# A row and its mirror image in one pass: first product shared between rows n and S-n, with the matmul order written out by hand

## The chip, the cores and the metric

The kernel runs on one core of a Trainium2 chip. A core has five engines, each with its own instruction queue that is served in order: PE (TensorE, matrix products; its weight loads are listed apart as PEld), DVE (VectorE), ACT (ScalarE), POOL (GpSimd) and SP (SyncE, which here only issues DMAs). Matrix products are written to PSUM, which has eight banks of 512 float32 columns in each of 128 partitions; everything else works from SBUF. The metric is the device time of one execution in microseconds; smaller is better.

## The reference

Input `x` is 8 batches of S = 3136 rows by 256 channels in float32. A two-dimensional Fourier transform is taken of each batch, and its real part goes through a mixer:

```
X = np.fft.fft(np.fft.fft(x, axis=1), axis=2).real      # rows, then channels
h = X.transpose(0, 2, 1) @ U @ V                         # rank 32 over the rows
u = X + h.transpose(0, 2, 1)
out = u + np.maximum(u @ w_ch1, 0) @ w_ch2               # 256 -> 1024 -> 256
```

For real input, X of row S-n is X of row n with the channels reversed (channel k and channel 256-k exchanged). The kernels use that.

## The kernel before, in words

**Layout.** Channels lie on partitions, rows on the free axis. Channels 1 to 127 and their mirror images 129 to 255 are kept as two halves of 128 partitions, so X of a batch is two tiles, `S` and `T`, of 128 partitions by 1569 columns: rows 0 to 1568 only. For row n the lower half is `S[:, n]` and the upper half `T[:, n]`; for row S-n the two change places. `W1[:, 0, :]` and `W1[:, 1, :]` hold the rows of `w_ch1` for the two halves (the second in the mirrored order).

**Transform of a batch** (`transform`, lines 669 to 678). `fold(b)` forms sums and differences of the loaded rows: DVE and POOL work in nine steps, of which `along_d` (L371, L373), `mirror` (L381, L384), `half` (L389) and `fourth` (L393) are the DVE ones. `load_x` brings the next batch into `xf` and `xr`, which exist once. Then come eight `seq` steps (L451): matmuls of 98 or 99 rows against cosine and sine tables into a PSUM tile of tag `dft`. In the first of each pair ACT copies the PSUM tile away (L467), in the second DVE combines it with that copy into `A` or `B` (`join`, L498 to L509; a POOL instruction, L512, turns the sign of one partition of `B`). Eight `chan` steps follow (two matmuls of 392 columns each, L567 and L569, and an ACT copy into `S` or `T`, L574), then `lowrank` (four matmuls of 256 columns, and two ACT copies into `TA`) and `mirror_row` (two DVE instructions on one partition, L588 and L590).

**The mixer** goes over all 25088 rows in 49 chunks of 512. `front(c)` adds the rank-32 part: two matmuls on 64 rows each of `TA` and `VA` (`s=0` on partitions 0 to 63, `s=1` on 64 to 127), into two PSUM tiles of tag `dft`; DVE adds `S` or `T` (L622) and writes `u`; a DMA from SP transposes `u` into `ut` (L625). `first_product(c, j)`, for j = 0 to 7, is two matmuls of 512 columns into a PSUM tile of tag `p1` and one ACT relu into `h` (L634, L636). `second_product(c, t)`, for t = 0 to 3, is eight matmuls of 256 columns into PSUM (tag `p2`, two t in one tile), after each pair three DVE adds with `ut` into `o` (L656, L658, L659), and after the fourth t a store of 512 rows.

**PSUM.** Of the eight banks, tag `dft` has three, `p1` three and `p2` two.

**Order.** Everything up to chunk 0, j = 3, with `front(1)` as its last step, is in the order of the text (`manual_schedule`). From there (`order.close()`, L851) a planner puts the instructions of each engine in order by its own estimate of when they are ready. The loop at L848 gives it, for each j of each chunk, first `first_product(c, j)`, then a tile of `second_product(c-1)`, then the steps of `transform(b)` due at that place (`due`); a batch's steps are spread evenly over the chunks of the batch before it. Chunk 0 begins once the first half of batch 0's `S` and `T` is there; `fold(1)` is the first thing that DVE does after the hand-ordered part.

**Set-up.** Before the loop: tables of sines and cosines, the transform of U, batch 0's transform, and the constants. POOL issues the loads of V into `VA`, clears its other rows (L199, L763), and casts `w_ch1` (L782).

Of the kernel before, what the change touches and what calls it, by code (L numbers as in the profile page):

```python
# [16 lines left out]
P = 128  # L17
# [14 lines left out]
def kernel(  # L32
# [16 lines left out]
    NCH = B * S // CH  # L49
# [48 lines left out]
    BUFS = {"dft": 3, "p1": 3, "p2": 2}  # L98
# [4 lines left out]
    UA = cpool.tile([KP, 4, NI, R], FP32, name="ua")  # L103
    J = cpool.tile([KP, KP], FP32, name="jx")
    jv = cpool.tile([KP, KP], FP32, name="jv")
    UR = cpool.tile([KP, 4, NI, R], FP32, name="ur")
    xidx = cpool.tile([P, B, 4], I32, name="xidx")
    krow = cpool.tile([P, 4 * NT], FP32, name="krow")
    kev = cpool.tile([P, 2 * NT], FP32, name="kev")
# [21 lines left out]
    lrow = cpool.tile([P, 2, P], FP32, name="lrow")  # L131
# [38 lines left out]
    VA = [cpool.tile([P, S], BF16, name=f"va{s}", tag=f"va{s}") for s in range(2)]  # L170
    TA = [cpool.tile([P, P], BF16, name=f"ta{s}", tag=f"ta{s}") for s in range(2)]
    MSN = cpool.tile([P, 256], BF16, name="msn")
    MC = cpool.tile([P, 256], BF16, name="mc")
    wp = ctx.enter_context(tc.tile_pool(name="wp", bufs=2))
    setup = ExitStack()
    gen = setup.enter_context(tc.tile_pool(name="gen", bufs=2))
# [14 lines left out]
    def cosine(out_, y, bits):  # L191
        pp = y.shape[0]
        ab = gen.tile(list(y.shape), FP32, tag="ab", name="ab")
# [4 lines left out]
    for r in (R, 3 * R):  # L198
        nc.gpsimd.memset(VA[0][r:r + R].bitcast(I32), 0)  # L199
# [5 lines left out]
    uy = cpool.tile([KP, 2, 2, 2, NI * R], FP32, name="uy")  # L205
    ueven = cpool.tile([KP, 2, 2, NI * R], FP32, name="ueven")
    GUO = cpool.tile([KP, 2, 2, NI, R], BF16, name="guo")
    GUC = [cpool.tile([KP, 2, NI, R], BF16, name=f"guc{c}", tag=f"guc{c}") for c in range(2)]

    NUO = cpool.tile([KP, 2, 2, R], BF16, name="nuo")  # L210
    NUC = [cpool.tile([KP, 2, R], BF16, name=f"nuc{c}", tag=f"nuc{c}") for c in range(2)]
# [185 lines left out]

    def fold(b):
# [50 lines left out]
    def add_up(pt, mm):  # L449
        for n, (at, w, rhs) in enumerate(mm):  # L450
            nc.tensor.matmul(pt[:, at:at + rhs.shape[-1]], w, rhs, start=(n == 0),  # L451
                             stop=(n == len(mm) - 1), skip_group_check=True)

    def seq(b, par, typ, pn, tag="dft", part=True):
# [5 lines left out]
        mm = products(b, par, typ, P * typ, pn == 1, ne)  # L460
        if typ == 0:
            mm = mm + products(b, par, 1, 256, (pn == 1) == (par == 1), ne)
        add_up(pt, mm)
# [51 lines left out]
    def seq_both(b, typ, tag, between):  # L515
# [3 lines left out]
        for pn in range(2):  # L519
            mm = products(b, 0, typ, P * typ, pn == 1, 0)  # L520
            if typ == 0:
                mm = mm + products(b, 0, 1, 256, pn == 0, 0)
            for n, (at, w, rhs) in enumerate(mm):
                nc.tensor.matmul(pt[:, at:at + rhs.shape[-1]], w, rhs, start=(pn == 0 and n == 0),
                                 stop=(n == len(mm) - 1), skip_group_check=True)
# [17 lines left out]
    def u_alone(b, typ, kept):  # L543
# [3 lines left out]
        mm = []  # L547
        for t, col in ((1, P),) if typ else ((0, 0), (1, 256)):
            for c in range(2):
                g = GC[b % 2][0 if (c == 0) == (t == 1) else 1]  # L550
                lo = TE - NT + NE * c
                mm += [(g[:kp(i), i, col:col + P], TABE[t][:kp(i), i, lo:lo + NE]) for i in range(NI)]
            for i in range(NI):
                tab, lo = (TABS[t], off_u(t, i)) if i % 2 else (TABO[t], 2 * NT)
                mm += [(GO[b % 2][:kp(i), nm, i, col:col + P], tab[:kp(i), nm, i // 2, lo:lo + NE])
                       for nm in range(2)]
        for n, (w, rhs) in enumerate(mm):
            nc.tensor.matmul(kept["pt"][:, typ, :], w, rhs, start=(n == 0), stop=(n == len(mm) - 1))
# [3 lines left out]
    def chan(b, ch, h, tag="dft"):  # L562
# [4 lines left out]
        nc.tensor.matmul(pt[:, :hi - lo], MC[:, h * P:(h + 1) * P], d["A"][:, lo:hi],  # L567
                         start=True, stop=False)
        nc.tensor.matmul(pt[:, :hi - lo], MSN[:, h * P:(h + 1) * P], d["B"][:, lo:hi],  # L569
                         start=False, stop=True)  # L570
# [5 lines left out]
    def lowrank(b):  # L576
        d = ST[b]
        pt = psum.tile([P, 256], FP32, tag="dft", name="ptt", bufs=3)
        parts = [(typ, par) for typ in range(2) for par in range(2 if b else 1)]
        for n, (typ, par) in enumerate(parts):  # L580
            nc.tensor.matmul(pt[:], d["tab"][:, typ, par, :], MDT[typ][:],
                             start=(n == 0), stop=(n == len(parts) - 1))
# [3 lines left out]
    def mirror_row(b):  # L586
        d = ST[b]
        nc.vector.tensor_tensor(VA[b % 2][R:R + 1, HALF + 1:S], d["S"][0:1, HALF - 1:0:-1],  # L588
                                d["T"][0:1, HALF - 1:0:-1], op=AL.subtract)
        nc.vector.tensor_copy(VA[b % 2][3 * R:3 * R + 1, HALF + 1:S], VA[b % 2][R:R + 1, HALF + 1:S])  # L590

    def pieces(c):
# [3 lines left out]
        while r < (c + 1) * CH:  # L596
            b, n = divmod(r, S)
            end = min((c + 1) * CH - b * S, S, HALF + 1 if n <= HALF else S)
            cuts.append((b, n, end, r - c * CH))
            r = b * S + end  # L600
        return cuts

# [288 lines left out]
```

## Time and profile before

| | |
|---|---|
| median of 3 runs | 483.94 us (483.89 to 483.95) |
| the profiled execution | 484.73 us, of which its span 482.9 us |
| granted clock of TensorE, mean | 0.982 |
| PE busy | 454.1 us, 94% of the span |
| DVE busy | 344.9 us, 71% |
| ACT busy | 281.2 us, 58% |
| POOL busy | 89.4 us, 19% |
| first `first_product` matmul starts | 42.13 us |

Matmuls overlap in the pipeline, so their times must not be added as they stand: a matmul of 256 columns lasts 273 ns in the group line, but a run of eight starts at 304.35 us and the next matmul's turn comes 0.87 us later. The spacing of starts is what a matmul costs PE.

### The profile page before, as it was taken

The page shows a single profiled execution, that of the slowest core. Times are in us where ns is not written, and L with a number is a line of the kernel's source. Part 1 is how long each engine was busy: PE and PEld are TensorE (multiplying, and loading weights), DVE is VectorE, ACT ScalarE, POOL GpSimd, SP SyncE. Part 2 cuts the span into 40 slices and gives each one's busy share as a digit, 9 for nine tenths or more (in the row PEclk, how much of TensorE's full clock was granted, in tenths as well). Part 3 has the DMA queues.
Part 4 walks back from the last instruction along what each step waited for, and adds up shares of the span by engine and source line. Part 5 has one row for each costly group of instructions (what it writes and reads, how often), then busy time and mean ns, then how long its engine had stood idle before and what let it go on. Part 6 is the DMA issues. An engine that isn't in the chain of part 4 may idle for free.

```text
span 482.9 us, 8346 instructions
## 1 busy us (share of the span) xinstructions
PE 454.1 (94%) x3137; PEld 296.2 (61%) x3192; DVE 344.9 (71%) x757; ACT 281.2 (58%) x560; POOL 89.4 (19%) x115
## 2 busy tenths in 40 slices
PE   2897699999999999999999999999999999999997
PEld 0573356656656675666756676666766676666665
DVE  8958989999999999996994457344634473534433
ACT  5936435756556554756556655755476555655552
POOL 8836402313053323330010001000010001000000
PEclk9959989999999999999999999999999999999999
DMA  5999393899938985687323332433224333243433
GB/s 158 242 219 154 92 259 104 168 267 220 245 75 224 224 223 189 147 227 225 67 67 87 111 88 65 110 85 112 67 70 115 94 81 98 70 115 93 121 96 123
DMA packets 87646, 67.55 MB, mean 140 GB/s; under 512 B 53890, under 2 KB 80918, under 8 KB 87606
## 3 DMA queue, kind: packets, MB, share of 16 engines
q1 hardware_dynamic: 81990, 52.06, 42.9%
q0 software_dynamic: 5616, 14.96, 12.3%
q8 instruction: 25, 0.41, 0.4%
q14 instruction: 15, 0.12, 0.1%
HBM read 30.06 MB, written 25.69 MB: 115 GB/s over the span
## 4 chain that ended last, share of the span: by engine, by line
PE 72%; DVE 20%; issue 3%; ACT 3%; DVEq 0%
PE p L650 30%; PE p L634 28%; PE pt L451 6%; PE ph L612 2%; DVE u L622 2%; PE pst L567 2%; PE pst L569 2%; DVE eor L373 2%; DVE o L659 1%; DVE B L498 1%; DVE eof L371 1%; DVE B L506 1%; DVE o L658 1%; DVE A L498 1%; DVE eor L371 1%
## 5 line engine op out<-in xcount | busy, mean ns | idle before, releaser
L636 ACT ACTIVATE h<-p 128x512 bf16<-128x512 f32 x392 | 218.7, 597 | 142.3 <-PE p L634 116.2
L650 PE MATMUL p<-w,h 128*128 128x256 bf16 x1568 | 204.6, 273 | 5.9 <-DVE o L659 4.9
L634 PE MATMUL p<-u,w 128*128 128x512 bf16 x729 | 203.2, 381 | 3.4 <-DVE u L622 1.3
L650 PEld LDWEIGHTS <-h 128*128 128x128 bf16 x1568 | 153.4, 98 | 65.2 <-DVE o L659 5.5
L634 PEld LDWEIGHTS <-w 128*128 128x128 bf16 x784 | 73.0, 98 | 58.5 <-issue 13.3
L656 DVE TENSOR_TENSOR o<-p,ut 128x4 f32<-128x4 f32 (+1 forms) x100 | 16.0, 160 | 105.4 <-PE p L650 105.3
L56 POOL DMA_INDIRECT xf<-in_x_dram,xidx x32 | 42.2, 1319 | 62.5 <-DVE eof L373 40.7
L512 POOL TENSOR_SCALAR B<-B 1x392 bf16<-1x392 bf16 x8 | 11.1, 1393 | 183.7 <-PE p L634 104.0
L658 DVE TENSOR_TENSOR o<-p,ut 128x254 f32<-128x254 f32 (+1 forms) x100 | 40.5, 405 | 0.0
L659 DVE TENSOR_TENSOR o<-p,ut 128x254 f32<-128x254 f32 (+1 forms) x100 | 40.5, 405 | 0.0
L622 DVE TENSOR_TENSOR u<-ph,S 128x512 bf16<-128x512 f32 (+15 forms) x64 | 34.9, 555 | 0.1
L622 DVE TENSOR_TENSOR u<-ph,T 128x512 bf16<-128x512 f32 (+15 forms) x64 | 34.8, 554 | 0.0
L467 ACT COPY ev<-pt 128x425 f32<-128x425 f32 (+2 forms) x30 | 15.4, 514 | 20.2 <-PE pt L451 20.2
L451 PEld LDWEIGHTS <-go 98*128 98x128 bf16 x192 | 19.4, 101 | 8.7 <-issue 1.2
L567 PE MATMUL pst<-A,mc 128*128 128x392 bf16 (+1 forms) x64 | 21.1, 330 | 3.6 <-DVE tab L509 1.8
L451 PE MATMUL pt<-te,gc 98*128 98x228 bf16 (+3 forms) x168 | 21.2, 262 | 0.5 <-DVE tab L509 0.3
L574 ACT CAST S<-pst 128x392 bf16<-128x392 f32 (+1 forms) x32 | 15.6, 488 | 9.9 <-PE pst L569 8.9
L569 PE MATMUL pst<-B,msn 128*128 128x392 bf16 (+1 forms) x64 | 21.1, 330 | 0.0
L451 PE MATMUL pt<-to,go 98*128 98x424 bf16 (+1 forms) x96 | 21.0, 357 | 0.0
L612 PE MATMUL ph<-va,ta 64*128 64x512 bf16 (+18 forms) x128 | 19.6, 334 | 0.2 <-ACT S L574 0.2
L373 DVE TENSOR_TENSOR eor<-xr 99x1016 bf16<-99x1016 f32 x16 | 19.6, 1228 | 0.0
L451 PEld LDWEIGHTS <-gc 98*128 98x128 bf16 (+1 forms) x168 | 15.8, 97 | 5.8 <-DVE tab L509 3.2
(140 smaller groups left out, 380.7 us busy)
## 6 DMA issues: line engine op xcount, KB each, us to landing
out_dram<-o SPq DMA_DIRECT2D x48, 512.0 KB
xr<-in_x_dram SPq DMA_DIRECT2D x7, 1568.0 KB
xr<-in_x_dram SPq DMA_DIRECT2D x2, 784.0 KB
va<-in_moe_V_dram POOLq DMA_DIRECT2D x4, 196.0 KB, 5.4
ut<-u SPq DMA_TRANSPOSE x49
xf<-in_x_dram,xidx POOLq DMA_INDIRECT x32, 6.6
w<-in_moe_w_ch_dram POOLq DMA_DIRECT2D x1, 512.0 KB
out_dram<-o SPq DMA_DIRECT2D x4, 128.0 KB
```

What stands on the lines that cost most here:

```text
L56: nc.gpsimd.indirect_dma_start(out_, None, bass.AP(t.tensor, t.offset, [[w, rows], [1, w]]), bass.IndirectOffsetOnAxis(idx, 0), element_of ...
L373: nc.vector.tensor_tensor(dst[:, qs, :, 129:256], lo, hi, op=AL.add)
L451: nc.tensor.matmul(pt[:, at:at + rhs.shape[-1]], w, rhs, start=(n == 0), stop=(n == len(mm) - 1), skip_group_check=True)
L567: nc.tensor.matmul(pt[:, :hi - lo], MC[:, h * P:(h + 1) * P], d["A"][:, lo:hi], start=True, stop=False)
L569: nc.tensor.matmul(pt[:, :hi - lo], MSN[:, h * P:(h + 1) * P], d["B"][:, lo:hi], start=False, stop=True)
L612: nc.tensor.matmul(phs[s][:, col:col + hi - lo], TA[b % 2][rows, :], VA[b % 2][rows, lo:hi], start=True, stop=True)
L622: nc.vector.tensor_tensor(u[:, s, col:col + hi - lo], ph[:, col:col + hi - lo], src, op=AL.add)
L634: nc.tensor.matmul(p1[:], W1[:, s, j * P:(j + 1) * P], k["u"][:, s, :], start=(s == 0), stop=(s == 1))
L636: nc.scalar.activation(k["h"][:, j, :], p1[:], AF.Relu)
L650: nc.tensor.matmul(p2[:, t % w, :], h[:, j, rs], W2[:, j, :], start=(j == 0), stop=(j == JT - 1))
L658: nc.vector.tensor_tensor(o[:, ts, 1:P], p2[:, :w, 1:P], ut[:, ts, 1:P], op=AL.add)
L659: nc.vector.tensor_tensor(o[:, ts, P + 1:D], p2[:, :w, P + 1:D], ut[:, tT, P - 1:0:-1], op=AL.add)
```

## The change

The mixer goes over rows n = 0 to 1567 of each batch, in 25 chunks of 512 (the last has 256), and does rows n and S-n of a chunk together.

- **First product.** `direct(c, q)` computes four of the eight j for rows n, as before (two matmuls of 512 columns each), into four `p1` banks, and ACT writes the relus. `mirrors(c, q)` then adds, in the same four banks, what turns the product of row n into that of row S-n: one matmul a bank with `WD` = `W1[:, 1]` - `W1[:, 0]` against `uo` = `S` - `T`, and one matmul of 32 rows a bank with `QF` against `DV`, the four of them on four different groups of 32 rows of the array. ACT then writes the relus of these, read backwards.
- **What that needs.** `QF` = `w_ch1` times the rank-32 factors of the batch: `lowrank(b)` copies all of its result into `TA` (two ACT copies), a DMA from SP transposes it into `TD`, POOL copies one partition of it, and `hidden(b)` makes `QF` with four matmuls of 512 columns and two ACT copies. `DV` = the difference of V's columns n and S-n, made once in set-up by two POOL instructions of 64 partitions by 1567; `WD` by one POOL instruction. `uo` is one more DVE instruction per chunk.
- **Front.** `front(c, hf)` is done for each half: matmuls of 32 rows in place of 64, one pair for rows n (`hf` = 0) and one for rows S-n (`hf` = 1). `mirror_row` and the clearing of `VA` and `TA` go; V is loaded by eight smaller DMAs in place of four. The middle rows (n = 1568) of the eight batches are gathered in `UH` and done at the end of the last chunk.
- **Stores.** One per half chunk, cut where a batch ends.
- **PSUM.** `dft` has two banks, `p1` four, `p2` two.
- **Order.** After the hand-ordered part, which now ends behind `front(1, 0)`, every matmul is held in the order of the text (`mm`, `keep_in_program_order`). The other engines are still ordered by the planner. The transform of batch b is put into the eight turns before its first use (five for batch 1), its fold into earlier turns.
- Several set-up tiles move from the lasting pool to the one that is closed before the loop.

```diff
-    BUFS = {"dft": 3, "p1": 3, "p2": 2}
+    BUFS = {"dft": 2, "p1": 4, "p2": 2}
...
+    def mm(*a, **k):
+        ins = nc.tensor.matmul(*a, **k)
+        if len(pinned) > 1:
+            tc.keep_in_program_order(ins)
+        if pinned:
+            pinned.append(ins)
...
     def lowrank(b):
...
-        for h in range(2):
-            nc.scalar.copy(TA[b % 2][2 * h * R:(2 * h + 1) * R, :], pt[2 * h * R:(2 * h + 1) * R, h * P:(h + 1) * P])
+        ta, td = TA[b % 2], TD[b % 2]
+        nc.scalar.copy(ta[:], pt[:])
+        nc.scalar.copy(ta[2 * R:, 0:P + 1:P], pt[2 * R:, P::-P])
+        nc.sync.dma_start_transpose(out=td[:], in_=ta[:])
+        nc.gpsimd.tensor_copy(td[0:1, :, 2 * R:], td[0:1, :, 0:2 * R])
+
+    def hidden(b):
+        for hh in range(2):
+            pt = psum.tile([P, CH], FP32, tag="dft", name="pq", bufs=BUFS["dft"])
+            for s in range(2):
+                mm(pt[:], TD[b % 2][:, s, :], W1[:, s, hh * CH:(hh + 1) * CH], start=(s == 0), stop=(s == 1))
+            nc.scalar.copy(QF[b % 2][:, hh * CH:(hh + 1) * CH], pt[:])
...
+    def front(c, hf):
...
+            for s in range(2):
+                rows = slice((2 * hf + s) * R, (2 * hf + s + 1) * R)
+                mm(phs[s][:, at:at + hi - lo], TA[b % 2][rows, s * P:(s + 1) * P], VP[rows, v:v + hi - lo],
+                   start=True, stop=True)
...
+            uo = k["uo"] = cp.tile([P, CH], BF16, tag="uo", name="uo", bufs=2)
+            for b, lo, hi, col in pieces(c):
+                nc.vector.tensor_tensor(uo[:, col:col + hi - lo], ST[b]["S"][:, lo:hi], ST[b]["T"][:, lo:hi],
+                                        op=AL.subtract)
...
+    def direct(c, q):
...
+        for j in range(4 * q, 4 * q + 4):
+            p1 = psum.tile([P, CH], FP32, tag="p1", name="p1", bufs=BUFS["p1"])
+            k["p1"].append(p1)
+            for s in range(2):
+                mm(p1[:, :w], W1[:, s, j * P:(j + 1) * P], k["u", 0][:, s, :w], start=(s == 0), stop=(s == 1))
+            nc.scalar.activation(k["h", 0][q][:, j - 4 * q, :w], p1[:, :w], AF.Relu)
+
+    def mirrors(c, q):
...
+        for g in range(4):
+            j = 4 * q + g
+            mm(k["p1"][g][:, :w], WD[:, j * P:(j + 1) * P], k["uo"][:, :w], start=False, stop=False,
+               skip_group_check=True)
+        for b, lo, hi, col in pieces(c):
+            for g in range(4):
+                j, rows = 4 * q + g, slice(g * R, (g + 1) * R)
+                mm(k["p1"][g][:, col:col + hi - lo], QF[b % 2][rows, j * P:(j + 1) * P], DV[rows, lo:hi],
+                   start=False, stop=True, skip_group_check=True)
+        for g in range(4):
+            nc.scalar.activation(k["h", 1][q][:, g, :w], k["p1"][g][:, :w][:, ::-1], AF.Relu)
...
     def transform(b):
+        steps = []
         for par, typ in [(0, 1), (0, 0), (1, 1), (1, 0)]:
+            steps.append(lambda par=par, typ=typ: seq(b, par, typ, 0))
+            steps.append(lambda par=par, typ=typ: (seq(b, par, typ, 1), join(b, par, typ)))
         for ch in range(4):
+            steps += [lambda ch=ch, h=h: chan(b, ch, h) for h in range(2)]
+            if ch == 1:
+                steps.append(lambda: lowrank(b))
+        steps.append(lambda: hidden(b))
+        return steps
...
+    nc.gpsimd.tensor_tensor(WD[:], W1[:, 1, :], W1[:, 0, :], op=AL.subtract)
...
     load_0(x, xf, xr, 1, D)
+    nc.gpsimd.memset(DV[:, 0:1], 0.0)
+    nc.gpsimd.tensor_copy(VP[2 * R:, HALF:HALF + 1], VP[2 * R:, 0:1])
+    nc.gpsimd.tensor_tensor(DV[:2 * R, 1:], VR[:2 * R, HALF - 1:0:-1], VP[:2 * R, 1:HALF], op=AL.subtract)
+    nc.gpsimd.tensor_tensor(DV[2 * R:, 1:], VP[2 * R:, HALF - 1:0:-1], VR[2 * R:, 1:], op=AL.subtract)
     setup.close()
...
+    put(0, lambda: chan(0, 2, 0), lambda: chan(0, 2, 1), lambda: hidden(0))
+    put(1, lambda: chan(0, 3, 0), lambda: chan(0, 3, 1))
+    done = 1
     for b in range(1, B):
+        end = 4 * (b * HALF // CH - 1) + 1
+        lo, done = max(done, end - 20), max(5, end - 11)
+        spread_out(list(fold(b)) + ([lambda b=b: load_x(b + 1)] if b + 1 < B else []), lo, done)
+        spread_out(transform(b), max(4, end - 8), end)
+    for c in range(NCH):
+        more = c + 1 < NCH
+        def turn(slot):
+            for step in due.get(4 * c + slot, []):
                 step()
+        direct(c, 0)
+        turn(0)
+        if c:
+            second_product(c - 1, 0, 2)
+            store(c - 1, 0)
+        mirrors(c, 0)
+        if more:
+            front(c + 1, 0)
+        if c == 0:
+            order.close()
+            tc.no_sync_barrier()
+            pinned.append(None)
+        else:
+            second_product(c - 1, 1, 0)
+        turn(1)
+        direct(c, 1)
+        if c:
+            second_product(c - 1, 1, 2)
+            store(c - 1, 1)
+        else:
+            front(0, 1)
+        turn(2)
+        mirrors(c, 1)
+        if more:
+            front(c + 1, 1)
+        second_product(c, 0, 0)
+        turn(3)
```

Here `second_product(c, hf, t0)` does two tiles of 128 rows, sixteen matmuls of 256 columns. The four `turn` calls of a chunk are the places of the transform's steps.

More of the change, by code (lines that the diff above doesn't have):

```diff
@@ L197 @@
     zeros(nc.gpsimd, 0)
-    for r in (R, 3 * R):
-        nc.gpsimd.memset(VA[0][r:r + R].bitcast(I32), 0)
+    zeros(nc.gpsimd, 1)
     for q in (0, 2, 1, 3):
@@ new lines, in blocks @@
+    def blocks(c, hf):
+        for b, lo, hi, col in pieces(c):
+            if hf:
+                lo, col, hi = max(lo, 1), col + (lo == 0), hi
+                at = width(c) - col - hi + lo
+                r0 = b * S + S - hi + 1
+            else:
+                at, r0 = col, b * S + lo
+            r0, end = r0 - at, at + hi - lo
+            while at < end:
+                p = at % P
+                np_, nt = (P, (end - at) // P) if p == 0 and end - at >= P else (min(P - p, end - at), 1)
+                yield r0 + at, p, np_, at // P, nt
+                at += np_ * nt
@@ L772 @@
     alone(OD, xf, EOF_)
-    for r in (0, 2 * R):
-        nc.gpsimd.dma_start(out=VA[0][r:r + R, :], in_=moe_V)
     nc.gpsimd.dma_start(out=W2[:], in_=moe_w_ch2.rearrange("(j p) d -> p j d", p=P))
@@ L848, with put @@
-    for c in range(NCH + 1):
-        for j in range(JT):
-            if (c, j) == (0, 4):
-                order.close()
-                tc.no_sync_barrier()
-            if c < NCH:
-                first_product(c, j)
-            if c > 0 and j % 2 == 1:
-                second_product(c - 1, j // 2)
-            for step in due.get(8 * c + j, []):
-                step()
-            if j == 3 and c + 1 < NCH:
-                front(c + 1)
+    due = {}
+    def put(slot, *steps):
+        due.setdefault(slot, []).extend(steps)
```

278 lines of the change are left out of this document (138 added, 140 removed).

## The prediction

> **What bounds the kernel now.** First the page: busy shares, and the slices of the span for PE and DVE.
>
> ```profile
> PE 454.1 (94%) x3137; PEld 296.2 (61%) x3192; DVE 344.9 (71%) x757; ACT 281.2 (58%) x560; POOL 89.4 (19%) x115
> ...
> PE   2897699999999999999999999999999999999997
> ...
> DVE  8958989999999999996994457344634473534433
> ```
>
> PE is full from about 60 us to the end; DVE is full as well until about 250 us and half idle after. Then the busy times by stretch (columns: stretch, its length, PE, weight loads, DVE, ACT, POOL, clock):
>
> ```profile
> 42.00:60.60 18.60, 12.96 (x74) 6.95 (x75) 17.13 (x24) 9.38 (x18) 8.97 (x13) 0.93 0.53 100
> 60.60:132.00 71.40, 70.08 (x472) 45.61 (x482) 68.75 (x135) 39.90 (x77) 14.64 (x21) 0.97 0.84 212
> 132.00:252.00 120.00, 117.21 (x806) 76.45 (x818) 114.40 (x222) 71.73 (x139) 32.68 (x28) 1.00 0.67 168
> ```
>
> The planner has DVE fold batches ahead of need, and PE hardly suffers. PE's own waits say where it does:
>
> ```profile
> PE p L650 <- DVE o L659: 4.9, 1, 4.9
> PE pst L567 <- DVE tab L509: 1.8, 3, 0.8
> PE p L634 <- DVE u L622: 1.3, 3, 0.8
> ```
>
> The 4.9 us are at 55.7 to 60.6 us, where DVE works off `fold(1)` (from 47.28 us) before it adds up the first outputs. Last, PE's order in time around one front:
>
> ```profile
> 303.92 0.59 PE L634 MATMUL p<-u,w 128*128 128x512 bf16 x2
> 304.35 1.04 PE L650 MATMUL p<-w,h 128*128 128x256 bf16 x8
> 305.32 0.39 PE L612 MATMUL ph<-va,ta 64*128 64x512 bf16 x2
> 305.64 0.39 PE L634 MATMUL p<-u,w 128*128 128x512 bf16 x1
> ```
>
> Two matmuls of 512 columns take 0.433 us (303.92 to 304.35), eight of 256 take 0.87, so about 0.1 us lies idle ahead of 305.32. The two 64-row matmuls both start at 305.32 and the next full one at 305.64: they ran together, 0.217 us, with another 0.1 us behind them. A front thus costs 0.42 us, half of it the two changes between full and part array. Where a batch ends, four of them of 64 and 448 columns (98.16 to 98.48) also took 0.32: further pieces cost nothing.
>
> **The change, part by part: PE's work.** Before, a chunk is 8 x 0.433 + 4 x 0.87 + 0.42 = 7.37 us; the starts at 439.93 and 447.31 in the chain agree. 49 chunks are 361.1. A transform has 20616 columns in 68 matmuls, 8.75 us at the spacings above; seven are 61.3; batch 0's last `chan` steps 1.3. From the first `first_product` at 42.13 an unbroken PE would end at 465.8. It ends at about 479.2: 4.9 are the stall, 2.1 the clock of 0.97 behind it, 6.4 the rest.
>
> After, a chunk of 1024 rows has 16 x 0.2167 for `direct`, 8 x 0.2167 for `WD`, 64 matmuls of 256 (6.96), and twice a part-array stretch: quarters 0.217, front 0.217 next to it, 0.2 for the changes. That is 13.4 against 14.74. The row for four 32-row matmuls is missing; between fully together (0.217, as the pairs did) and in turn (0.867) I take the first. (The Trainium skill, "TensorE: Matmul & The Clock Gate", Part 3 on packing small matmuls, gives 3.07 times for four row tiles, not 4; by it a quartet would take an estimated 0.28 us and the sum would be 3 us longer. No run here shows it yet.) Chunk 0 is 8.6, the 23 full ones 308.5, the half one with the middle rows 12.9, `hidden` 8 x 0.867 = 6.9, transforms and `chan` as before: 399.5. Unbroken, PE would end at 441.6, **24.2 us earlier**. What is left to cost is waits.
>
> **Beside the path.** `uo`: by the 965 ns of `mirror_row`'s 1567 columns some 0.33 us x 25; `mirror_row` itself (L588, L590: 12.2 us) goes; DVE's total stays. ACT gains two 512-column copies and one of 256 a batch, about 10 us on 58%: beside PE, except where named below. Four more V loads on POOL (0.56 us each) and the `WD` instruction stand near a 6.9 us wait of POOL for the `w_ch1` gather; uncovered they would delay the next `xf` gathers by 3 us, which `fold(1)` needs only at 47. Some 20 more stores on SP at 0.4 us each stand ahead of `ut` transposes that are needed over 5 us later; uncovered, outputs would hold the `p2` banks and so PE. Set-up tiles closed early cost nothing unless a loop tile on their place waits for `DV` to be read: 0 to 3 us, within the bounds below.
>
> **The start.** The hand-ordered part now ends behind `mirrors(0, 0)` and `front(1, 0)`, and DVE can't begin `fold(1)` before that front's adds. `mirrors(0, 0)` needs `DV` and `QF`. `lowrank`'s ACT copies end near 39.4, SP then issues the transpose; its landing has no row, so between 1.2 (the issue alone) and 6.6 (a gather's) I take 4: 43.5. On POOL, in order: the copy into `TD`, the sign of `B` (1.39, and `chan(0, 2, ..)` waits for it), a memset and a copy: 45.4. Then `DV`, two of 1567 elements. POOL rows give from 1.0 ns an element (L782, 1037 ns for 1024) to 3.5 (L512, 1393 ns for 392); I take the middle, 3.5 us each: 52.4. (The Trainium skill, "GPSIMD Engine Reference", 3.1 on elementwise cycle accounting, has some 2.6 cycles an element for two inputs; by it an estimated 3.4 us each, and the same sum.) Quarters and front end at 52.8, adds and `uo` at 54.6, and DVE then has fold 15.0 (eight of 1.13, four of 0.6, two of 1.17, two of 0.6) and, ahead of its end, the adds of two more fronts and a cast, 2.9. `fold(1)` ends at 72.5. PE meanwhile does all of chunk 0 and `direct(1, 0)`, 12.6 us of work, and then stands in its given order before batch 1's first `seq`, which needs the last fold step; in before the planner let it go on with chunk work. Lost: 72.5 - 54.7 = 17.8 us; bounds 13.7 (landing 1.2, 1.0 ns; then `QF` is last, 48.5) and 24.4. The clock after it I take as in before, 2.1 (0 to 2.4).
>
> **The transforms.** With PE's order fixed and two `dft` banks, what follows a step waits for ACT or DVE to empty a bank. In the rows ACT and DVE start 0.2 us behind PE, PE goes on 0.05 behind them. By turns, DVE idle: `seq(0,0)` behind the copy of `seq(0,1)` (0.51): 0.37. `front(c+1, 1)`, 1.4 us behind a `seq` whose `join` is 1.93 (0.82, 0.05, 0.83, 0.23): 0.6. `chan(0,0)` directly behind the last `seq`, whose `join` must write `B` (0.58): 0.66, less a matmul. Third `chan` of a turn behind the copy of the first (0.49): 0.40. `hidden`'s second half behind a `chan` copy that queues after four relus (0.55 each): 0.85. Sum 2.9 a batch, 20.3 for seven. Before the same places cost about 0.8 a batch (5.5 us behind 60.6, the clock apart), which is the lower bound: 5; the upper adds a fold instruction (1.13) in front of DVE at two of them and half at the others: 4.5, or 31.
>
> **A full DVE.** Until some 250 us folds run ahead again and every `dft` and `p2` bank is emptied between them; also the `TD` chain (ACT 0.6, issue 1.2, landing 4, POOL) has only 5.7 us of PE work over it, and POOL stood up to 15.6 us at an `xf` gather. In before all this is in the 0.8. I take 3 us, bounds 0 and 10.
>
> **The end.** The last two tiles are added together (0.73 against 0.45) and stored at once: 4.3 us behind PE's end against 3.7.
>
> Sum: 441.6 + 17.8 + 2.1 + 20.3 + 3 + 4.3 = 489.1, as a span. The profiled execution took 484.73 with a span of 482.9, the median is 483.94, 1.0 above that span: **490 us**, 1.3% slower.
>
> **Rivals.** (1) Faster: the bank waits in the transforms stay what they were, 0.8 a batch, because ACT and DVE empty in an order that suits PE. For it: ACT idles 142 us before relus, and DVE is half idle behind 250. Against: two banks, not three, and no other matmul may go ahead. It gives 490 - 15 = 475, and it decides below 2.0 us a batch (6.2 us less than my sum); with the start's lower bound, a constant clock and no harm from DVE, 466. (2) The quarters run in turn: 49 x 0.65 = 32 us more, 522, and the change saves no PE work at all. For it: no four-row-group row; against: the pairs started together. (3) The start's hole is as in before, because `fold(1)` does not wait: 12 us less than 17.8 leaves 478; the hand order speaks against. It goes with (1).
>
> **Numbers.** No change can be told within 0.2% (1 us). The forecast case, 485 to 515 by its bounds, has 0.61; (1) and (3), 465 to 483, 0.32; (2) 0.04; within 0.2% 0.03. Two in ten may be left out, but both signs hold much, so the range takes both: 465 to 515.
>
> **What would show it.** In the profile after: four 32-row matmuls starting together; first products with some 138 us of PE in place of 170; PE idle before batch 1's first `seq` at about 60 to 72 us with the fold as releaser; PE waits on DVE `B` and on ACT copies in each transform. I am wrong if that first `seq` starts before 66, or if PE's waits behind it stay under 10 us; wrong the other way if quarters start one after another or `hidden` waits for `TD`.

## The result and the profile after

The changed kernel takes 535.69 us (median of 4 runs, 534.35 to 539.82) against 483.94 us before: a ratio of 1.108, 95% interval 1.102 to 1.114. The forecast was 490 us and its range ended at 515: the direction was right, the size was not. The profiled execution took 535.21 us with a span of 533.4 us; the forecast as a span was 489.1, so 44.3 us are to be found.

The page of the changed kernel: busy shares, then PE, DVE and the granted clock in 40 slices of 13.3 us.

```profile
PE 460.0 (86%) x3304; PEld 292.2 (55%) x3304; DVE 344.4 (65%) x786; ACT 281.2 (53%) x584; POOL 112.0 (21%) x142
...
PE   4781675966988899899999999979999999999995
...
DVE  8950499894998869997777367515743474344432
...
PEclk9775675896999989999999999979999999999999
```

PE is no longer full. Its row has holes in the fourth to seventh slice, in the ninth and tenth, and in the twenty-seventh; the clock is low beside or behind each of them. The busy total (460.0 against 454.1) does not show that PE has less to do; the spacing of starts does. All matrix products now stand in the helper `mm`, line 407, so they are told apart by their tiles. PE's order in time over one half chunk, where nothing waits:

```profile
491.46 1.03 PE L407 MATMUL p<-uo,wd 128*128 128x512 bf16 x4
492.42 0.40 PE L407 MATMUL p<-dv,qf 32*128 32x512 bf16 x4
492.64 0.38 PE L407 MATMUL ph<-vp,ta 32*128 32x512 bf16 x2
492.95 1.92 PE L407 MATMUL p<-w,h 128*128 128x256 bf16 x16
```

The four quarters start at 492.42 and the front 0.22 us later: the four ran together. From 492.95 to the same place of the next half chunk, 499.69, are 6.74 us, so a chunk of 1024 rows costs PE 13.48 us against 14.74 before. What the change was to save, it saves.

The waits of PE in the changed kernel (waiting tile and line, releaser: us in total, times, longest):

```profile
PE pq L407 <- POOL td L599: 16.1, 4, 9.0
PE p L407 <- DVE u L649: 15.4, 1, 15.4
PE pst L407 <- DVE B L513: 5.9, 7, 1.4
PE pt L407 <- DVE gc L399: 5.6, 1, 5.6
PE ph L407 <- DVE tab L524: 4.1, 6, 2.2
```

The first two had no term of that size in the forecast. The second is at the start. In order of time, on DVE and PE:

```profile
56.18 0.69 DVE L649 TENSOR_TENSOR u<-ph,S 128x512 bf16<-128x512 f32 x1 [15.33 <-POOL dv L907]
```
```profile
56.93 3.74 PE L407 MATMUL p<-u,w 128*128 128x512 bf16 x8 [15.44 <-DVE u L649]
```

The first `u` of the loop needs nothing of `DV`. It waits for POOL's second `DV` instruction all the same, and the first product starts at 56.93 us in place of 42.13. The other wait comes where a batch's `hidden` needs `TD`. In the transform of batch 5, on SP, POOL and PE:

```profile
344.92 2.15 SPq L598 DMA_TRANSPOSE td<-ta  x1
...
352.92 0.28 POOL L599 COPY td<-td 1x128 bf16<-1x128 bf16 x1 [17.05 <-DMA td<-ta]
```
```profile
353.25 1.89 PE L407 MATMUL pq<-w,td 128*128 128x512 bf16 x4 [3.32 <-POOL td L599]
```

From the issue of the transpose of `TD` to POOL's copy of its result are 8.0 us, and POOL had been idle for 17 us: that is the landing. `hidden` stands in PE's given order and nothing may go ahead of it. The longest of these waits, 9.0 us, is in batch 1:

```profile
115.43 4.42 SPq L598 DMA_TRANSPOSE td<-ta  x1
...
124.19 0.28 POOL L599 COPY td<-td 1x128 bf16<-1x128 bf16 x1 [2.80 <-DMA td<-ta]
```

The issue alone takes 4.42 us there. Over batches 1 to 7, from the start of the issue to the copy took 8.8, 6.6, 4.1, 4.2, 8.0, 2.5 and 2.4 us, and each time the copy was released by that DMA. Four of the seven made PE wait: batches 1, 2, 3 and 5.

Last, the stretches from batch 1's first `seq` to the next batch's, and so on to batch 7's (columns: stretch, length, PE, weight loads, DVE, ACT, POOL, clock, DMA share, GB/s):

```profile
85.93:147.03 61.10, 50.32 (x322) 31.12 (x323) 51.35 (x97) 25.89 (x52) 20.02 (x21) 0.83 0.76 176
147.03:209.14 62.11, 55.19 (x385) 34.68 (x385) 53.87 (x107) 32.12 (x64) 22.74 (x21) 0.95 0.74 183
209.14:263.76 54.62, 51.62 (x385) 33.15 (x384) 47.40 (x99) 31.77 (x64) 11.87 (x14) 1.00 0.63 159
263.76:316.80 53.04, 51.47 (x387) 33.17 (x384) 32.43 (x84) 31.90 (x65) 2.96 (x4) 1.00 0.41 91
316.80:375.38 58.58, 53.91 (x386) 34.36 (x384) 28.87 (x79) 31.91 (x65) 2.96 (x4) 0.94 0.40 83
375.38:428.31 52.93, 51.10 (x386) 33.34 (x384) 26.69 (x76) 31.81 (x65) 1.95 (x4) 1.00 0.38 91
```

By the forecast's terms a stretch is three chunks of 13.4, a transform of 8.75, `hidden` of 0.87 and bank waits of 2.9, together 52.7; the first, nine turns and not twelve, is 42.7. Two of the six come out as that, within 0.4 us. The others are too long by 18.4, 9.4, 1.9 and 5.9 us. With the 0.5 of the two good ones that is 36.1 us, where the forecast had 5.1 (2.1 for the clock, 3 for a full DVE and the chain of `TD`). The first `seq` itself starts at 85.93, forecast 72.5: 13.4 more. 13.4 and 31.0 are the 44.3, to the roundings.

### The profile page after: what moved, and what is told of

It reads as the page before. It is cut to its first block, busy times and chain, and to the rows that moved or that the text cites. A ratio compares the mean times of both kernels' runs of the same rounds, so it can differ in the third digit from the quotient of the medians.

```text
span 533.4 us, 8819 instructions
## 1 busy us (share of the span) xinstructions
PE 460.0 (86%) x3304; PEld 292.2 (55%) x3304; DVE 344.4 (65%) x786; ACT 281.2 (53%) x584; POOL 112.0 (21%) x142
## 4 chain that ended last, share of the span: by engine, by line
PE 58%; DVE 20%; DMA 9%; issue 5%; POOL 4%; ACT 3%; SPq 1%; DVEq 0%; POOLq 0%
PE p L407 46%; PE pt L407 6%; DMA xf<-in_x_dram,xidx 4%; DVE u L649 3%; DMA td<-ta 2%; PE pst L407 2%; PE ph L407 2%; DVE eor L379 2%; DVE eor L377 2%; POOL xf L57 2%; DMA xr<-in_x_dram 2%; PE pq L407 2%; DVE eof L379 1%; DVE o L744 1%; DVE o L745 1%
## 5 line engine op out<-in xcount | busy, mean ns | idle before, releaser
L698 ACT ACTIVATE h<-p 128x512 bf16<-128x512 f32 (+1 forms) x200 | 101.5, 595 | 97.7 <-PE p L407 95.5
L682 ACT ACTIVATE h<-p 128x512 bf16<-128x512 f32 (+1 forms) x200 | 102.1, 596 | 37.9 <-PE p L407 37.7
L407 PE MATMUL p<-u,w 128*128 128x512 bf16 (+1 forms) x400 | 95.3, 382 | 15.4 <-DVE u L649 15.4
L742 DVE TENSOR_TENSOR o<-p,ut 128x4 f32<-128x4 f32 x99 | 16.1, 163 | 126.1 <-PE p L407 123.7
L407 PEld LDWEIGHTS <-w 128*128 128x128 bf16 x400 | 39.4, 99 | 55.2 <-issue 19.2
L649 DVE TENSOR_TENSOR u<-ph,S 128x512 bf16<-128x512 f32 (+9 forms) x64 | 35.1, 560 | 27.7 <-POOL dv L907 15.3
L407 PE MATMUL p<-uo,wd 128*128 128x512 bf16 (+1 forms) x200 | 51.8, 382 | 0.0
L482 ACT COPY ev<-pt 128x425 f32<-128x425 f32 (+2 forms) x30 | 15.4, 514 | 48.6 <-PE pt L407 48.6
L745 DVE TENSOR_TENSOR o<-p,ut 128x254 f32<-128x254 f32 x99 | 40.7, 411 | 0.0
L744 DVE TENSOR_TENSOR o<-p,ut 128x254 f32<-128x254 f32 x99 | 40.7, 411 | 0.0
L527 POOL TENSOR_SCALAR B<-B 1x392 bf16<-1x392 bf16 x8 | 16.1, 2016 | 111.9 <-DVE tab L524 88.3
L649 DVE TENSOR_TENSOR u<-ph,T 128x512 bf16<-128x512 f32 (+9 forms) x64 | 35.0, 559 | 1.6 <-PE ph L407 0.9
L407 PE MATMUL pt<-te,gc 98*128 98x229 bf16 (+1 forms) x192 | 25.9, 280 | 7.6 <-DVE gc L399 5.6
L407 PE MATMUL ph<-vp,ta 32*128 32x512 bf16 (+15 forms) x128 | 22.7, 332 | 7.6 <-DVE tab L524 4.1
L407 PEld LDWEIGHTS <-gc 98*128 98x128 bf16 x216 | 20.6, 104 | 12.4 <-DVE gc L399 6.5
L407 PE MATMUL pq<-w,td 128*128 128x512 bf16 x32 | 11.1, 458 | 17.5 <-POOL td L599 16.1
```

The lines of the kernel that those rows point to most:

```text
L407: ins = nc.tensor.matmul(*a, **k)
L482: nc.scalar.copy(ev[:, :w], pt[:, :w])
L527: nc.gpsimd.tensor_single_scalar(dst[0:1, 785:HALF:2], dst[0:1, 785:HALF:2], -1.0, op=AL.mult)
L649: nc.vector.tensor_tensor(u[:, s, at:at + hi - lo], phs[s][:, at:at + hi - lo], src, op=AL.add)
L682: nc.scalar.activation(k["h", 0][q][:, j - 4 * q, :w], p1[:, :w], AF.Relu)
L698: nc.scalar.activation(k["h", 1][q][:, g, :w], k["p1"][g][:, :w][:, ::-1], AF.Relu)
```

## The experiments

Each was compared with runs of the kernel before on the same chip; their medians were 484.43 us for the `e` runs, 485.94 for `g`, 486.66 for `h`, and 484.36 for `i` and `j`. Where the gain of one step over another is told, it is between runs on one chip unless two groups are named.

**The two waits.** The theory: the first `u` lies on the place in memory that the set-up tile `VR` leaves, and `DV` is the last to read `VR`. One run keeps `VR` in the lasting pool, and nothing else.

```diff
-    VR = gen.tile([P, HALF], BF16, name="vr")
+    VR = cpool.tile([P, HALF], BF16, name="vr")
```

> Only the tile VR moves to the pool that lasts, so that no tile of the loop lies on its place. Theory (the first front's adds waited for DV only because u lies where VR lay): the first first_product starts near 41.5 us instead of 56.9; DV itself still ends near 56, so the quarters of mirrors(0, 0) come near 56.4 instead of 64.0 and everything behind them moves by that 8 us: about 527 us. Rival 1 (the whole 15 us wait is what it costs): about 520. Rival 2 (the gate is elsewhere, the wait only changes its name): 535.

The second makes `TD` without a DMA: PE forms it (eight matmuls of 128 columns more a batch), ACT copies it.

```diff
-        nc.sync.dma_start_transpose(out=td[:], in_=ta[:])
-        nc.gpsimd.tensor_copy(td[0:1, :, 2 * R:], td[0:1, :, 0:2 * R])
+        qt = psum.tile([P, 2, P], FP32, tag="dft", name="ptd", bufs=BUFS["dft"])
+        for s in range(2):
+            for n, (typ, par) in enumerate(parts):
+                mm(qt[:, s, :], MDT[typ][:, s * P:(s + 1) * P], d["tab"][:, typ, par, :],
+                   start=(n == 0), stop=(n == len(parts) - 1))
+        nc.scalar.copy(td[:], qt[:])
```

> TD comes straight from PE (eight matmuls of 128 columns with the operands changed round, one ACT copy), in place of the transposing DMA and the POOL copy. Theory (hidden stands in PE's given order behind a transfer that lands late, and PE's clock falls after each long wait): the four waits of 16 us in sum go, about 8 us of low clock with them, and 8 x 0.45 us of matmuls come: about 514 us, clock above 0.95. Rival (PE then waits as long at the same place for a bank or for ACT): 530 or more, with waits on ACT in front of hidden.

> Both edits. Theory: the two are at different places and add up, 535 - 8 - 21 = about 506 us. Rival (both are cover for one later gate, the fold of batch 1 on DVE and the banks): no better than the better of the two alone, 514.

Measured: 526.34 us with `VR` kept (1.086, 1.081 to 1.091), 521.43 with `TD` by PE (1.076, 1.070 to 1.082), 514.58 with both (1.062, 1.057 to 1.067). PE's waits, of `e1_vr_kept` and then of `e2_td_by_pe`:

```profile
PE pq L407 <- POOL td L599: 18.5, 4, 9.5
PE pt L407 <- DVE gc L399: 8.0, 1, 8.0
```
```profile
PE p L407 <- DVE u L653: 17.3, 1, 17.3
```

Each edit took away its own wait and left the other's. Against the changed kernel's 535.69, a comparison over two groups, the edits give 9.4 and 14.3 us alone and 21.1 together, where 8, 21 and 29 were expected. A wait of 15.4 us gave only 9.4 because the next gate was close behind: with `VR` kept the quarters still wait for `DV`, and the wait before batch 1's first `seq` grows from 5.6 to 8.0. The 16.1 us of `TD` and the low clock behind them gave 14.3, between theory and rival: the edit costs something too, since a late batch takes 53.75 us with it and 52.9 without. `e3_both` was expected at 506 and came out at 514.6. That is the number of its rival and not its reason: `e3_both` is 6.9 us better than the better of the two alone, so the edits do nearly add up, and 506 was missed mostly because `TD` had been priced too high. In `e3_both` PE still stands before that `seq`:

```profile
80.19 3.47 PE L407 MATMUL pt<-te,gc 98*128 98x229 bf16 x16 [8.03 <-DVE gc L399]
```

and from batch to batch it takes 53.4, 57.1, 56.0 and then 53.8 us.

**The given order.** The same kernel, with PE's order left to the planner:

```diff
-        if len(pinned) > 1:
-            tc.keep_in_program_order(ins)
```

> Both edits, and the matmuls are not held in the order of the text: the planner orders PE as it did before. Theory (given order with two dft banks costs 2.9 us a batch in waits, and a hole in front of batch 1's transform): up to 30 us less than with both edits, about 480. Rival (the planner's order is worse, because the shared p1 banks and two dft banks leave it nothing to go ahead with): more than 506.

It took 497.66 us (1.027, 1.021 to 1.033): 16.9 less than `e3_both`. PE no longer waits for batch 1's `gc`; it does chunk 1 meanwhile. The expected 480 was missed: 8.0 us of waits for the `DV` instructions stay, and the second and third stretch still take 57.5 and 55.3 us against 52.1 late, which I put down to a full DVE. The same edit alone, in the changed kernel, was tried last:

> The changed kernel (535.7 us) with PE's order left to the planner, and nothing else undone. Theory: VR's place and the TD chain stall PE whatever its order, since all of chunk 0 stands behind the first u, but the planner puts chunk work in front of hidden and of batch 1's first seq: 17 us of order as between e3_both and e4_both_free_order, and some more for TD, about 513 us. Rival: most of the td waits go too, and the kernel is near 505 us; or, the other way, the order gives under 10 us here, because the stalls hide it: 526 us or more.

It took 511.57 us (1.054, 1.049 to 1.058), as the theory had it. The 17.2 us wait for the first `u` is there in any order, and 10.7 us of waits for `TD` as well.

**`DV` earlier.** V's loads ahead of those of `W2`, and the two `DV` instructions ahead of the cast of `w_ch1` on POOL.

```diff
+    for g in range(4):
+        near, far = (VP, VR) if g < 2 else (VR, VP)
+        nc.gpsimd.dma_start(out=near[g * R:(g + 1) * R, 0:HALF], in_=moe_V[:, 0:HALF])
+        nc.gpsimd.dma_start(out=far[g * R:(g + 1) * R, 0:HALF], in_=moe_V[:, HALF:S])
     nc.gpsimd.dma_start(out=W2[:], in_=moe_w_ch2.rearrange("(j p) d -> p j d", p=P))
...
+    nc.gpsimd.tensor_tensor(DV[:2 * R, 1:], VR[:2 * R, HALF - 1:0:-1], VP[:2 * R, 1:HALF], op=AL.subtract)
+    nc.gpsimd.tensor_tensor(DV[2 * R:, 1:], VP[2 * R:, HALF - 1:0:-1], VR[2 * R:, 1:], op=AL.subtract)
     nc.gpsimd.tensor_copy(W1[:, 1, :], w1t[:])
```

> As with both edits (VR kept, TD by PE), and V is loaded ahead of w_ch2 and DV is made on POOL ahead of the cast of w_ch1. Theory (the hand-ordered part ends when DV is there, and fold of batch 1 and all of PE's given order shift with it): the quarters of mirrors(0, 0) start near 48.5 us instead of 55.3 and 58.2, the fold near 50.5 instead of 60.5, and the time falls by 10 us to about 504. Rival (PE in its low clock of the start, or the fold, is what lasts): less than 4 us.

> The same with the planner's order of matmuls. Theory: with early DV the planner has chunk work until the fold ends; 497.7 - 8 = about 490. Rival (DVE, full until about 250 us, is the limit of the first half, so an earlier start is waited away again): 495 or more.

Both missed: 520.92 us (1.073, 1.067 to 1.079) and 500.77 (1.031, 1.026 to 1.037). Against the kernels without the edit, of another group, the first is slower (1.073 against 1.062); for the second (1.031 against 1.027) the intervals overlap. The first `u` on DVE in `g1_both_dv_early` says why:

```profile
51.10 0.69 DVE L653 TENSOR_TENSOR u<-ph,S 128x512 bf16<-128x512 f32 x1 [9.17 <-POOL w L862]
```

Line 862 there is the cast that reads `w1t`, another set-up tile. `u` needs nothing of `w_ch1`. The reading is that with `VR` gone from the place, `u` waits for the last reader of the tile beside it, which the edit had put later on POOL; in `e1_vr_kept` the first `u` waits 0.51 us for the same cast. No view shows the tiles' places, but this is the same fault as `VR`'s in another tile, and it agrees with the reading of the first one.

**The transforms' places.** The eighteen steps of a transform laid out over twelve turns and not eight, so that no step stands directly behind the one whose bank it needs.

```diff
-        return steps
+        return {end - 8: sq[0:2], end - 7: sq[2:3], end - 6: sq[3:5], end - 5: sq[5:7], end - 4: sq[7:8],
+                end - 3: ch[0:1], end - 2: ch[1:3], end - 1: [ch[3], low], end: ch[6:8], end + 1: ch[4:5],
+                end + 2: ch[5:6], end + 3: [hid]}
```

> The given order kept, with DV early, and the transform's 18 steps laid out over twelve turns so that no step needs a bank that was filled less than 1.2 us before (for batch 1: over eight turns, one turn later than before). Theory (the waits of 2.9 us a batch are the two dft banks and the steps that stand directly behind their producers): 7 x 2.4 = 17 us less than the 504 expected with DV early, and some 3 us less of the hole before batch 1's transform: about 484. Rival (what PE loses in the given order is DVE being late in the first half): 498 or more, with the waits behind 250 us gone all the same.

> The same layout of steps, with the planner's order of matmuls. Theory: the layout takes away what the planner had to work round, so this is within 5 us of the given order with the same layout. Rival: the planner moves steps together again and lands where it was without the layout, about 490.

With the given order 504.0 us (1.038, 1.034 to 1.042), 16.9 less than `g1_both_dv_early`; with a free order 496.41 (1.022, 1.015 to 1.029), 4.4 less than `g2_dv_early_free_order`. The gain of 17 is what was expected; the times were not, since `g1_both_dv_early` itself had come out 17 us late, and the free order is 7.6 us better than the given one, not within 5. With the given order a batch takes 51.2 us in place of 53.8 behind 250 us. So the bank waits were at least 2.6 us a batch there. In the second and third stretch, where DVE is full, the layout gives only 1.0 and 0.7 us, which is the rival's point; another 3.0 lie in the first stretch and 3.0 behind batch 7's first `seq`.

**The start.** V is loaded by four DMAs into one tile, ahead of `W2`; `DV` is one DVE instruction of 128 partitions; and `front(1, 0)` goes ahead of `mirrors(0, 0)`, so that DVE need not wait for the quarters before it can begin `fold(1)`.

```diff
-    VP = cpool.tile([P, HALF + 1], BF16, name="vp")
-    VR = cpool.tile([P, HALF], BF16, name="vr")
+    VV = cpool.tile([P, S + 1], BF16, name="vv")
...
+    for g in range(4):
+        nc.gpsimd.dma_start(out=VV[g * R:(g + 1) * R, 0:S], in_=moe_V[:, :])
...
+    nc.vector.tensor_tensor(DV[:, 1:], VV[:, S - 1:HALF:-1], VV[:, 1:HALF], op=AL.subtract)
...
-        mirrors(c, 0)
+        if c:
+            mirrors(c, 0)
         if more:
             front(c + 1, 0)
         if c == 0:
+            mirrors(c, 0)
```

> VR kept and TD made by PE, as in e3_both (514.6 us), and the start changed: V loaded by four DMAs in place of eight, ahead of the load of W2, into one tile; DV made by one DVE instruction of 128 partitions in place of two of 64 on POOL; front(1, 0) ahead of mirrors(0, 0). Theory: in e3_both PE waits 2.5 + 2.3 us for DV's instructions and 8.0 us before batch 1's first seq, because DVE can't begin fold(1) (60.5 us) before the quarters have run; with fold(1) beginning near 50 both waits go and the time is about 502 us. Rival: fold(1) is held by a full DVE or by the landing of its own loads, the end of its last step stays near 80 us, and the time is 511 us or more.

> h1_start with the eighteen steps of a transform laid out over twelve turns, as in g3_dv_early_spaced. The spacing gave 17 us there (520.9 to 504.0). Theory: the bank waits in the transforms are a cost of their own, independent of the start, and the two gains add: about 485 us. Rival: the spacing works only where DVE is not full, and a shorter start leaves less of it: 492 us or more.

> h2_start_spaced with PE's order left to the planner. Theory: the given order costs PE what is left of the waits in the first half, where DVE is full and the order can't be changed: about 479 us, faster than the kernel before (484 to 486). Rival: with start and spacing mended the given order costs nothing more: within 3 us of h2_start_spaced.

`h1_start` took 504.23 us (1.034, 1.028 to 1.041), 10.4 less than `e3_both` of another group. On DVE and then on PE:

```profile
45.06 0.98 DVE L912 TENSOR_TENSOR dv<-vv 128x1567 bf16<-128x1567 bf16 x1
...
50.40 1.21 DVE L376 TENSOR_TENSOR eof<-xf 99x1016 bf16<-99x1016 f32 x1
```
```profile
70.05 3.47 PE L406 MATMUL pt<-te,gc 98*128 98x229 bf16 x16 [8.03 <-DVE gc L398]
```

`fold(1)` begins at 50.40 in place of 60.53, and the first `seq` comes at 70.05 in place of 80.19: the gain is that shift. The wait before the `seq` is as long as it was, since PE's work in front of it moved too; the theory was right on the time and wrong in saying that this wait goes. `h2_start_spaced` took 491.52 (1.007, 1.003 to 1.011), 12.7 less and not 17: 0.5 from its rival. `h3_start_spaced_free` took 482.03 (0.989, 0.983 to 0.995), 9.5 less again, where the rival had 3 at most. It is 1.1% faster than the kernel before.

**Folds held.** Up to some 230 us a batch takes 57 us in `h2_start_spaced` (57.0, 57.3) and 51.2 behind. DVE was tried as the cause: the fold instructions of batches 2 to 7 are held in the order of the text, so that they can't run ahead of a chunk's adds. First with PE's order given, then free, then both with every fold instruction a step of its own.

```diff
+    def dve(*a, **k):
+        ins = nc.vector.tensor_tensor(*a, **k)
+        if held:
+            tc.keep_in_program_order(ins)
```

> h2_start_spaced with the fold instructions of batches 2 to 7 held on DVE in the order of the text, so that they can't run ahead of the adds of chunks that stand before them. Theory: PE's waits for DVE up to 250 us (u, tab, B) come of folds run early on a DVE that is 95% busy; held, DVE's work is even over the span and these waits go: 5 to 8 us faster than h2_start_spaced, about 479 us. Rival: the waits have other causes, or the folds then come late before the first seq of a batch: the same time or slower.

> h3_start_spaced_free (482.0 us) with the folds of batches 2 to 7 held on DVE in the order of the text. Theory: folds that run ahead cost batches 2 and 3 some 6 us each (57.6 and 56.0 us against 50.9 behind), held they cost 2 us at most each with PE free to pass: about 475 us. Rival: the free order already works round them: within 2 us of 482.

> h4_folds_held (488.3 us) with each fold instruction a step of its own, so that one of 1.2 us and not two or three stands in front of an add of u. Theory: the 9.7 us of PE's waits for u are what a held step's length costs, and they halve: about 483 us. Rival: the number of steps and not their length counts: within 2 us of 488.

> j1_held_free with the fine steps of j2_held_fine. Theory: some 51 us a batch throughout, about 472 us, 2 to 3% faster than the kernel before. Rival: as j1_held_free within 2 us.

Measured: 488.26 us (1.004, 1.001 to 1.007), 479.23 (0.989, 0.987 to 0.991), 487.56 (1.006, 1.003 to 1.009) and 477.80 (0.987, 0.984 to 0.991). A stretch of 53 us early and one late in `h2_start_spaced`, and then the same two in `h4_folds_held` (columns as above):

```profile
112.00:165.00 53.00, 48.67 (x370) 31.39 (x368) 51.83 (x101) 29.25 (x60) 24.07 (x20) 1.00 0.86 203
...
323.00:376.00 53.00, 52.51 (x410) 35.39 (x408) 27.04 (x76) 32.94 (x68) 1.67 (x3) 1.00 0.33 90
```
```profile
112.00:165.00 53.00, 50.96 (x393) 33.71 (x392) 41.02 (x93) 31.80 (x66) 7.69 (x11) 1.00 0.62 151
...
323.00:376.00 53.00, 50.95 (x394) 33.74 (x392) 40.96 (x92) 31.82 (x66) 2.57 (x4) 1.00 0.34 91
```

Free to run ahead, DVE is busy for 51.8 of 53 us early and for 27 late. Held, it has 41 in both, and every batch behind the first stretch takes 53.1 us: some 4 less than early, 1.9 more than late. The clock is 1.00 in all four lines, so it is not the clock. What differs is how full DVE is; POOL and the DMA share differ as well, but with DVE at 41 us a DMA share of 0.62 and one of 0.34 go with the same PE time. The net gain was 3.3 us and not the expected 5 to 8. Why the rest is not gained is not shown. That a held step's length costs it is not borne out by `j2_held_fine`: apart from the one in front of batch 1's first `seq`, PE's waits before a `seq` for an add of `u` were ten of 7.8 us in all in `h4_folds_held` and ten of 9.7 there. With a free order and held folds (`j1_held_free`) a batch takes 52.7 us throughout. The time is 2.8 us less than that of `h3_start_spaced_free`, between theory and rival, but the two groups differ, and against the kernel before the ratio is 0.989 in both: the times alone do not show this gain. Shorter steps change nothing that can be told, 0.7 us (over two groups) and 1.4, as the rivals had it. `j3_held_fine_free`, 1.3% faster than the kernel before, is the best that was reached.

## Why the prediction failed, step by step

**PE's work** was right: 13.48 us a chunk against 13.4, and four quarters in 0.22 us, the lower end of their bounds. Rival (2) falls. The Trainium skill, "TensorE: Matmul & The Clock Gate", Part 3, has 3.07 times for four row tiles; the trace does not agree, the four cost the 0.22 us of one.

**Beside the path.** The first step that failed is "Set-up tiles closed early cost nothing unless a loop tile on their place waits for `DV` to be read: 0 to 3 us, within the bounds below". The mechanism is named there and the size is wrong: the tile is the first `u`, not a later one, so all of the loop stood behind the end of `DV` at 56.15 us. `e1_vr_kept` shows it by moving one tile. The first fold instruction on DVE, in the changed kernel and then in `e1_vr_kept`:

```profile
66.27 1.21 DVE L377 TENSOR_TENSOR eof<-xf 99x1016 bf16<-99x1016 f32 x1
```
```profile
59.54 1.21 DVE L377 TENSOR_TENSOR eof<-xf 99x1016 bf16<-99x1016 f32 x1
```

From the end of `DV` to the fold are 10.1 us in the changed kernel, because the first half of chunk 0 and `front(1, 0)` come in between; with `VR` kept it is 2.3, and the forecast had 2.2. ACT, by the way, was not busier at all (281.2 us in both kernels), where 10 us were charged to it, beside the path.

**The start.** The hole was to be 17.8 us, 24.4 at most. By the same reckoning (12.6 us of work behind the first product at 42.13, against the first `seq` at 85.93) it was 31.2. Of the 13.4 us more, 7.9 are the tile on `VR`'s place, 3.8 the later end of `DV` and 1.8 the fold. The landing of `TD` played no part in it. `DV` cost less than forecast, 2.87 us an instruction and not 3.5, but started at 50.33 and not 45.4. POOL waited 2.47 us ahead of it for a transfer. The profile names a gather for `xf`, which nothing there reads; it may have been the last load of V, which went out at 38.52, and this is not shown. `fold(1)` then took 19.7 us, where 17.9 were charged. (The Trainium skill, "GPSIMD Engine Reference", 3.1 on elementwise cycle accounting, has some 2.6 cycles an element for two inputs, an estimated 3.4 us for a `DV` instruction; the trace is below it, at 2.87.)

**The clock** was a term of 2.1 us, "as in before". Behind 84 us alone it cost six times that. Windows of 6 us behind two of the changed kernel's waits, with the columns of the stretches above:

```profile
84.00:90.00 6.00, 3.43 (x16) 2.17 (x17) 6.00 (x9) 1.03 (x2) 5.68 (x2) 0.50 0.91 252
90.00:96.00 6.00, 6.00 (x27) 4.02 (x27) 4.58 (x10) 0.00 (x0) 3.30 (x5) 0.50 0.82 205
120.00:126.00 6.00, 1.47 (x4) 0.58 (x5) 1.89 (x3) 0.40 (x1) 2.70 (x4) 0.50 0.51 120
126.00:132.00 6.00, 6.00 (x34) 3.52 (x33) 2.90 (x7) 1.44 (x4) 3.25 (x4) 0.64 0.68 200
```

PE's busy time times the missing part of the clock is 7.6 us in these four windows; with four more at 156, 186, 348 and 354 us (0.72, 0.72, 0.85, 0.59) it is 12.9, an estimate by these windows. The shortest wait beside a low window is one of 2.17 us at 157.40. Behind the waits that end at 85.93, 124.53 and 353.25, PE's starts stay at double spacing for some 10, 6 and 6 us. The Trainium skill, "TensorE: Matmul & The Clock Gate", Part 1, has half the rate after at least one idle window of about 3.4 us; the trace agrees on the 0.50, and here shorter waits were enough. The forecast put new waits into the sum and left the clock behind them out.

**The transforms** were right. Behind 375 us the five places come 0.39, 0.77, 0.66, 0.40 and 0.65 us late, 2.87 in all against 2.9 forecast from 0.37, 0.6, 0.66, 0.40 and 0.85. Three of the five fit one by one; that the other two offset each other is luck. The largest that the trace names is the one of `chan(0,0)`:

```profile
391.53 0.33 PE L407 MATMUL pst<-B,msn 128*128 128x393 bf16 x1 [0.50 <-DVE B L513]
```

So rival (1) falls, and rival (3) with the hole.

**A full DVE** was a term of 3 us, bounds 0 and 10, with the chain of `TD` in it. It is the second step that failed. The chain had "issue 1.2, landing 4", 5.2 us together, for every batch. It took from 2.4 to 8.8, and in three of seven batches over 6.5, so that 5.7 us of PE work over it were not enough; in batch 3, at 4.1, PE waited 0.8. One middle value fits the median (4.2) and misses the cost, because a batch that lands early gives nothing back. These waits were 16.1 us, and `e2_td_by_pe` got 14.3 by taking them away. What makes the landing vary is not shown: the two longest issues, 4.4 and 2.2 us, go with the two longest times. The text named this as what would make it "wrong the other way" (`hidden` waits for `TD`) and gave it no more than the upper bound of 10 us for the whole term.

Of the 36.1 us that the stretches hold too much, 16.1 are this and 12.9 the clock; the remaining 7 I put down to the full DVE, which the later kernels support but no run isolates in the changed kernel itself. Its trace has one clear case: at 157.40 PE waits 2.17 us for `tab`, and DVE had worked off three fold instructions and three adds, from 151.27 to 155.38, in front of that `join`. Behind 375 us the same wait is 0.39.

**The end** was 5.4 us (PE's last product ends at 528.0), forecast 4.3; with it the terms add up to 1.2 us more than was found.

## What to carry to other kernels

A pool that is closed early hands its memory to the next tiles: for each set-up tile that is moved there, find its last reader and ask which of the first loop tiles lies on its place. A hand-written order turns every late operand into a stall of the engine, and on PE a long stall is paid again in clock (here an estimated 2.9 us behind one of 3.3): price a transfer in such a chain by the longest landing of that very transfer, not by a middle one, or make the operand on an engine that is in the order anyway. A planner's run-ahead has a price when the engine that it fills is the one that empties banks for another: here 4 us a batch early, against 1.9 us a batch late when the run-ahead was forbidden.

## What the runs showed of the hardware

Four matmuls of 32 rows on four quarters of the array took the time of one, 0.22 us for 512 columns.

A subtraction of 1567 bf16 columns, one input read backwards, took POOL 2.87 us for 64 partitions and DVE 0.98 us for 128, so `DV` cost 5.7 us in one place and 1.0 in the other.

A transpose of 128 x 256 by DMA, from SBUF to SBUF, took from 2.4 to 8.8 us from issue to use in seven batches of one kernel, 4.2 in the median.

Loads issued by POOL waited for the transfer eight places earlier; whether the chip or the program's own semaphores set the eight, no run shows. On POOL in `e3_both`, with the load of `W1` the first of nine:

```profile
18.09 0.66 POOL L844 DMA_DIRECT2D w<-in_moe_w_ch_dram  x1 [0.17 <-issue]
...
29.11 0.49 POOL L857 DMA_DIRECT2D vr<-in_moe_V_dram  x1 [2.19 <-DMA w<-in_moe_w_ch_dram]
```

Splitting V's four loads into eight therefore cost more than four issues: the last of them went out at 40.31 us, while in `h1_start` four loads ahead of `W2` were all out by 23.5.
